# Value means of the first two batches by TensorE products of untransposed values, and 1e-9 added to the early sums on GpSimd

## Chip, cores and metric

The kernel runs on one core of a Trainium2 chip. The metric is the device time of one execution in microseconds, the median of repeated runs. PE is TensorE, DVE is VectorE, ACT is ScalarE, POOL is GpSimd, SP is SyncE, whose queue issues most of the DMAs. An engine carries out its instructions strictly in the order of its queue.

## The reference: what is computed

Four batches, 8 heads, 768 positions, 64 values per head. Attention is a window of 31 positions around each query, joined with 24 summaries of the sequence: of each block of 32 positions the maximum of the keys and the mean of the values. The result goes through an FFN of width 1024: a product with `w_in`, relu, a depthwise convolution of 3 taps, a sigmoid gate, a product with `w_out`.

```python
nb = S // block                                   # 24 blocks of 32
k_sum = k.reshape(B, H, nb, block, D).max(axis=3)
v_sum = v.reshape(B, H, nb, block, D).mean(axis=3)
scores_l_m = np.where(mask_l, scale * q @ k.T, -1e9)
scores_s = scale * np.einsum('bhsd,bhnd->bhsn', q, k_sum) + np.log(block)
scores_all = np.concatenate([scores_l_m, scores_s], axis=-1)
a = np.exp(scores_all - scores_all.max(axis=-1, keepdims=True))
a = a / (np.sum(a, axis=-1, keepdims=True) + 1e-09)
x = np.matmul(a, np.concatenate([v, v_sum], axis=2))
h = np.maximum(x @ w_in, 0.0)
out = (h * sigmoid(conv3(h, conv_w))) @ w_out
```

## The kernel before

The work is cut into 8 chunks: chunk c is one half (384 positions) of batch c // 2. A chunk has 4 head pairs, and two heads of 64 values fill the 128 partitions. `n = 4 * c + p` counts the pairs from 0 to 31. For each pair:

- `prep_pair` (L201): the block maxima of the keys on DVE (`ks`, L209, in the first chunk of a batch), which POOL copies behind the window keys (L216).
- `vmean_pair` (L220), in the first chunk of a batch only: DVE sums the transposed values `vT` over blocks of 32 positions (`vs`, L227, 128 x 768 to 128 x 24), PE transposes the 24 columns into PSUM (`pv`, L233), ACT scales by 1/32 (`vm`, L235). In chunk 0 POOL spreads the means over the six blocks of `va` (L237); later they go there by DMA (L197). Batch 0's `vT` lies in `raw_b`, batches 1 to 3 use a staging tag of two buffers that the loads of `w_out` (L117) use as well.
- `qk` and `softmax` (L247, L270): for each of six blocks of 64 queries and each head one fp32 product of 64 x 120 scores on PE (L259); DVE scales, masks and takes the extreme in one instruction (L277, six per pair); ACT takes the exponential and sums (`sm`, L287, six per pair); ACT adds 1e-9 (L295), DVE takes the reciprocal (L296); the multiply of the weights by it is on DVE for chunk 0 and on POOL afterwards (L299, two per pair).
- `tr` and `av`: six PE transposes of the weights (L307), the copy to `aT` on ACT or DVE (L312, L314), then 12 products with `va` (L328) into `xp`, split into a high part `xh` (ACT) and a rest `xl` (DVE).

The FFN of a chunk has 8 units of 128 columns. `f1` (L403) makes 12 products per unit: four groups of 128 rows times the three combinations of high and low parts of `x` and `w_in`. Relu, taps and gate go to ACT and DVE; the gated result is split into `ghi` (ACT, L454) and `glo` (POOL, L455). `f2` (L471) multiplies by `w_out` the same way. The weights come as 64-bit words and are decoded by ACT and DVE (L96 to L103), split by ACT into the high part (L126) and by POOL into the low part `win_lo` or `wout_lo` (L127).

The attention of chunk c + 1 is woven into the units of chunk c: `slot(j)`, `slot_t(j)` and `slot_av(j)` are called once per unit. The pieces of `f2` are spread over later units by `work`. Around the start PE also runs fillers without use for the result (`warm`, L77, 128 x 512 bf16): 10 first, 5, 12, 3 and 3 behind the scores of chunk 0's pairs, two or three behind its transposes and products and behind chunk 0's units. A scheduler then fixes the order of each engine's queue from estimates of its own, so an edit moves instructions far beyond its own lines. The loads of keys, queries, values and `w_in` are issued on SP in the order of the string `LOADS`; mask and the identity are issued on ACT's queue. Loads for chunk 1 reuse the buffers of chunk 0's pairs and wait for these.

Of the kernel before, what the change touches and what calls it, by code (L numbers as in the profile page):

```python
# [7 lines left out]
F32 = mybir.dt.float32  # L8
F32R = mybir.dt.float32r
U32 = mybir.dt.uint32  # L10
AF = mybir.ActivationFunctionType
ALU = mybir.AluOpType
AX = mybir.AxisListType

B, H, S, D = 4, 8, 768, 64
DM, DF = 512, 1024
P = 128
WIN = 16
BLK = 32
NB = S // BLK  # L20
# [5 lines left out]
NP = H // 2  # L26
CH = S // 2
CB = CH // QB
# [13 lines left out]

OUT_AT = (6, 7, 8, 9, 10, 10, 11, 12)
WARM = {"start": 10, "pq0": 5, "pq1": 12, "pq2": 3, "pq3": 3, "tr": 2, "av": 3, "unit": 3}
EARLY_AT = 3
NGROUP = NCHUNK * NP * 2


@with_exitstack
def attention_ffn(ctx, tc, qT, kT, vT, v4, w_in, cwT, w_out, mask8, ident_in, out):  # L50
    nc = tc.nc
    cp = ctx.enter_context(tc.tile_pool(name="cp", bufs=1))
    sp = ctx.enter_context(tc.tile_pool(name="sp", bufs=2))
# [3 lines left out]
    mask = cp.tile([P, 2, 3, NK], F32, name="mask")  # L57
    ident = cp.tile([P, P], F32, name="ident")
    cw = cp.tile([P, NFC, 3], F32, name="cw")
    win_hi = cp.tile([P, NFC, NCC, P], F32R, name="win_hi")  # L60
    win_lo = cp.tile([P, NFC, NCC, P], F32R, name="win_lo")
    wout_hi = cp.tile([P, NFC, DM], F32R, name="wout_hi")
# [3 lines left out]
    raw_b = cp.tile([P, 6, 1024], U32, name="raw_b", tag="big_b")  # L66
# [7 lines left out]
    def warm(where, after=None):  # L74
        def go():
            for i in range(WARM.get(where, 0)):
                nc.tensor.matmul(pw, idle[:, :P], idle, start=True, stop=True)  # L77
# [55 lines left out]
    state = {}  # L133

    spare = []
    for tag in ("xh", "xl"):
        t = sp.tile([P, 2, KL], F32, tag=tag, name=f"k_{tag}", bufs=2)
# [31 lines left out]
    def load_vt(c, p):  # L169
        b, hf = divmod(c, 2)  # L170
        i = c * NP + p
        if hf:
            return
        if b == 0:
            v = raw_b[:, 2 + p, :S].bitcast(F32)
        else:
            v = sp.tile([P, 1024], F32, tag="stage", name=f"vt{i}", bufs=2)[:, :S]
        nc.sync.dma_start(v, vT[b, p])
        state[(c, p)]["vt"] = v

# [38 lines left out]

    def vmean_pair(c, p):  # L220

        b, hf = divmod(c, 2)
        if hf:
            return
        st = state[(c, p)]
        vs = sp.tile([P, NB], F32, tag="vs", name=f"vs{c}_{p}", bufs=2)
        nc.vector.tensor_reduce(  # L227
            vs, st["vt"].rearrange("p (n t) -> p n t", t=BLK), AX.X, ALU.add
        )
        pv = ps.tile(  # L230
            [P, 512], F32, tag="t" if c else "f1", name=f"pv{c}_{p}", bufs=1 if c else 3
        )
        nc.tensor.transpose(pv[:NB, :P], vs, ident)  # L233
        vm = cp.tile([NB, P], F32, tag=f"vm{p}", name=f"vm{c}_{p}")
        nc.scalar.activation(vm, pv[:NB, :P], AF.Copy, scale=1.0 / BLK)  # L235
        if c == 0:
            nc.gpsimd.tensor_copy(  # L237
                st["va"][WK:NK, :, :], vm.unsqueeze(1).to_broadcast([NB, CB, P])
            )
        state[("vm", b, p)] = vm  # L240
# [6 lines left out]
    def qk(c, p):  # L247


        st = state[(c, p)]  # L250
        n = c * NP + p
        pq = [
            ps.tile([P, 512], F32, tag="s", name=f"pq{n}_{h}", bufs=2) for h in range(2)
        ]
        for blk in range(CB):
            i, half = divmod(blk, 2)
            for h in range(2):
                r = slice(h * QB, (h + 1) * QB)
                last = nc.tensor.matmul(  # L259
                    pq[h][half * QB : (half + 1) * QB, i * NK : (i + 1) * NK],  # L260
                    st["q"][r, blk * QB : (blk + 1) * QB],
                    st["kw"][r, blk, :],
                    start=True,
                    stop=True,
                )
        if c == 0:
            warm(f"pq{p}", ins(last))
        softmax(n, c % 2, pq)

    def softmax(n, hf, pq):  # L270
        nm = sp.tile([P, 2, 3], F32, tag="nm", name=f"nm{n}", bufs=3)
        sm = sp.tile([P, 2, 3], F32, tag="sm", name=f"sm{n}", bufs=3)
        for h in range(2):
            a = sp.tile([P, 3, NK], F32, tag="a", name=f"a{n}_{h}", bufs=DEPTH + 2)
            state[("a", 2 * n + h)] = a
            for i in range(3):
                nc.vector.tensor_tensor_reduce(  # L277
                    a[:, i, :],
                    pq[h][:, i * NK : (i + 1) * NK],
                    mask[:, hf, i, :],  # L280
                    -0.125,
                    3.0e38,
                    ALU.add,
                    ALU.min,
                    nm[:, h, i : i + 1],
                )
                nc.scalar.activation(  # L287
                    a[:, i, :],
                    a[:, i, :],
                    AF.Exp,  # L290
                    bias=nm[:, h, i : i + 1],
                    scale=-1.0,
                    accum_out=sm[:, h, i : i + 1],
                )
        nc.scalar.activation(sm, sm, AF.Copy, bias=1e-9)  # L295
        nc.vector.reciprocal(sm, sm)  # L296
        for h in range(2):
            a = state[("a", 2 * n + h)]
            (nc.gpsimd if n >= NP else nc.vector).tensor_tensor(  # L299
                a, a, sm[:, h, :].unsqueeze(2).to_broadcast([P, 3, NK]), ALU.mult  # L300
            )
# [56 lines left out]
    def slot(j):  # L358

        if j % 2 == 0:  # L360
            n = j // 2 + 2
            if NP <= n < npair:
                load_k(*divmod(n, NP))
                load_vt(*divmod(n, NP))
            if NP <= j // 2 < npair:
                load_vm(*divmod(j // 2, NP))
            if j // 2 < npair:
                qk(*divmod(j // 2, NP))
        else:
            n = (j + 1) // 2  # L370
            if NP <= n + 1 < npair:
                load_q(*divmod(n + 1, NP))
            if n < npair:
                c, p = divmod(n, NP)
                if c:
                    vmean_pair(c, p)
                    load_v(c, p)
                prep_pair(c, p)
# [106 lines left out]
    cw_words = sp.tile([P, 2 * NFC * 3], U32, tag="cww", name="cw_words", bufs=1)  # L485
    nc.scalar.dma_start(mask, mask8)
    nc.scalar.dma_start(ident, ident_in)

    for item in LOADS.split():
        what, n = item[0], int(item[1:] or 0)  # L490
        if what == "k":
            load_k(0, n)
        elif what == "q":
            load_q(0, n)
        elif what == "v":
            load_vt(0, n)
        elif what == "a":
            load_v(0, n)
        elif what == "w":
            raws[n] = load_in(n)  # L500
        else:
            nc.sync.dma_start(cw_words, cwT.bitcast(U32))

    prep_pair(0, 0)
    for j in range(2 * NP):
        slot(j)
        if j % 2 == 0:
            vmean_pair(0, j // 2)
        slot_t(j)
        slot_av(j)  # L510
# [18 lines left out]
    def spread(x, n):  # L529
        return [x[len(x) * i // n : len(x) * (i + 1) // n] for i in range(n)]  # L530

    def work(c):
# [10 lines left out]
        if c == 1:  # L543
            return [[]] * EARLY_AT + spread(parts, NFC - EARLY_AT)
        return spread(parts, NFC)
# [111 lines left out]
```

## Time and profile before

| | |
|---|---|
| median of 3 runs | 415.49 us (414.77 to 416.97) |
| the profiled execution | 414.49 us, its span 412.7 us |
| mean granted clock of TensorE | 0.986 |
| block sums of values (L227) | 16 on DVE: 4 in batch 0 from 8.9 to 24.0 us, 12 from 59.8 to 252.2 us |
| their transposes (L233) | 16 on PE, 0.27 us each as recorded |
| 1e-9 added to the sums (L295) | 32 on ACT, 0.21 us each as recorded |
| fillers (L77) | 85 on PE |

The profile is one execution, recorded on the core. Times are in microseconds from the start of the span unless marked ns. PE is a matmul, PEld its weight load, SPq or ACTq the queue that issues DMAs on that engine. A row of a group reads: line, engine, operation, out<-in, shapes, count | busy time, mean ns of one | idle time of that engine just before them, with what ended it. Matmuls overlap in the pipeline, so the recorded length of one is more than what it adds to a sequence. Rows of the chain have start, duration and what ran; "issue" is time in which nothing shown was waited for.

### The profile page before, as it was taken

The numbers are of one execution on the slowest core, as the hardware profiler recorded it, in microseconds if no ns is written. First come the engines' busy times: TensorE is split into PE (matmuls) and PEld (weight loads), VectorE is DVE, ScalarE is ACT, GpSimd is POOL, SyncE is SP. The second block draws the span as 40 slices with busy tenths as digits, with TensorE's granted clock in tenths as the row PEclk, the third lists the DMA queues.
The fourth block names the chain that finished last, engine by engine and source line by source line (L and its number), as shares of the span: only waits on it lengthen the run. The fifth ranks groups of instructions, "written<-read, shape, count | busy, mean of one in ns | idle before, by whom it ended". The sixth has DMA issues, their size and how long they took to land.

```text
span 412.7 us, 8842 instructions
## 1 busy us (share of the span) xinstructions
PE 395.1 (96%) x3173; PEld 318.4 (77%) x3173; DVE 262.0 (63%) x777; ACT 255.9 (62%) x806; POOL 148.8 (36%) x179
## 2 busy tenths in 40 slices
PE   7989689998999999999999999999999999999996
PEld 3546458775878887888888788887888888888885
DVE  4898989999766756577665454565646655555400
ACT  3664999988695767766556667755666554334211
POOL 2325655565654323332243333333323322212200
PEclk9999999998799999999999999999999999999999
DMA  8999855857976764565332233333111000000011
GB/s 289 331 363 187 241 159 168 241 158 237 218 206 197 231 164 139 151 177 137 84 108 90 78 86 110 111 89 112 54 46 56 27 0 27 25 27 25 28 51 51
DMA packets 60715, 54.47 MB, mean 132 GB/s; under 512 B 24640, under 2 KB 51328, under 8 KB 60672
## 3 DMA queue, kind: packets, MB, share of 16 engines
q1 hardware_dynamic: 56928, 47.19, 40.0%
q10 hardware_dynamic: 3744, 6.73, 4.3%
q8 instruction: 25, 0.41, 0.4%
q14 instruction: 18, 0.15, 0.1%
HBM read 45.55 MB, written 6.29 MB: 126 GB/s over the span
## 4 chain that ended last, share of the span: by engine, by line
PE 74%; ACT 10%; DVE 6%; DMA 3%; POOL 2%; SPq 2%; issue 2%; ACTq 0%; DVEq 0%
PE f L471 30%; PE f L403 28%; PE pq L259 5%; PE xp L328 5%; ACT a L287 4%; PE pt L307 4%; DVE t L433 2%; PE pw L77 2%; DMA va<-v 1%; DMA k_xh<-kT 1%; ACT ob L480 1%; ACT t L424 1%; ACT f L421 1%; ACT aT L314 1%; POOL a L299 1%
## 5 line engine op out<-in xcount | busy, mean ns | idle before, releaser
L455 POOL TENSOR_TENSOR glo<-t,ghi 128x383 fp32r<-128x383 f32 (+1 forms) x64 | 64.9, 1015 | 133.6 <-ACT ghi L454 125.6
L403 PE MATMUL f<-xh,win_hi 128*128 128x384 f32 (+1 forms) x256 | 95.3, 372 | 0.2 <-DVE t L451 0.2
L433 DVE SCALAR_TENSOR_TENSOR t<-f,cw,t 128x382 f32<-128x382 f32 (+3 forms) x128 | 78.7, 615 | 17.1 <-ACT t L424 14.8
L403 PE MATMUL f<-xl,win_hi 128*128 128x384 f32 (+1 forms) x256 | 87.9, 343 | 0.0
L403 PE MATMUL f<-xh,win_lo 128*128 128x384 f32 (+1 forms) x256 | 87.2, 341 | 0.0
L471 PE MATMUL f<-wout_hi,ghi 128*128 128x512 f32 x192 | 79.3, 414 | 1.2 <-ACT ob L480 0.4
L287 ACT ACTIVATE a<-a,nm 128x120 f32<-128x120 f32 x192 | 73.3, 384 | 10.6 <-DVE nm L277 9.9
L471 PE MATMUL f<-wout_lo,ghi 128*128 128x512 f32 x192 | 76.0, 396 | 0.9 <-POOL wout_lo L127 0.8
L471 PE MATMUL f<-wout_hi,glo 128*128 128x512 f32 x192 | 75.3, 392 | 0.0
L450 ACT ACTIVATE t<-t 128x383 f32<-128x383 f32 (+1 forms) x64 | 33.4, 524 | 60.6 <-DVE t L433 60.1
L299 POOL TENSOR_TENSOR a<-a,sm 128x360 f32<-128x360 f32 x56 | 45.9, 840 | 48.3 <-ACT f L421 43.2
L403 PEld LDWEIGHTS f<-xh,win_hi 128*128 128x128 f32 x256 | 48.8, 190 | 7.7 <-issue 3.6
L451 DVE SCALAR_TENSOR_TENSOR t<-t,f 128x383 f32<-128x383 f32 (+1 forms) x64 | 35.4, 553 | 30.2 <-ACT t L450 30.2
L403 PEld LDWEIGHTS f<-xl,win_hi 128*128 128x128 f32 x256 | 49.0, 191 | 1.4
L403 PEld LDWEIGHTS f<-xh,win_lo 128*128 128x128 f32 x256 | 48.7, 190 | 0.4
L471 PEld LDWEIGHTS f<-wout_hi,ghi 128*128 128x128 f32 x192 | 36.1, 188 | 11.6 <-ACT ob L480 3.9
L454 ACT CAST ghi<-t 128x383 fp32r<-128x383 f32 (+1 forms) x64 | 32.8, 512 | 18.5 <-DVE t L451 18.3
L277 DVE CUSTOM_DVE_ANT_0 a<-pq,mask 128x120 f32<-128x120 f32 x192 | 42.4, 276 | 1.5 <-PE pq L259 1.5
L471 PEld LDWEIGHTS f<-wout_hi,glo 128*128 128x128 f32 x192 | 36.2, 188 | 7.8
L471 PEld LDWEIGHTS f<-wout_lo,ghi 128*128 128x128 f32 x192 | 36.2, 189 | 6.9 <-POOL wout_lo L127 1.6
L259 PEld LDWEIGHTS pq<-kw,q 64*64 64x64 f32 x768 | 24.2, 133 | 21.2 <-issue 12.1
L259 PE MATMUL pq<-kw,q 64*64 64x120 f32 x768 | 35.6, 276 | 4.3 <-issue 2.3
(59 smaller groups left out, 508.1 us busy)
## 6 DMA issues: line engine op xcount, KB each, us to landing
va<-v SPq DMA_DIRECT2D x32, 288.0 KB
kw<-kT SPq DMA_DIRECT2D x28, 288.0 KB
q<-qT SPq DMA_DIRECT2D x32, 192.0 KB
out_dram<-ob ACTq DMA_DIRECT2D x24, 256.0 KB
kT<-kT SPq DMA_DIRECT2D x12, 392.0 KB
vt<-vT SPq DMA_DIRECT2D x12, 384.0 KB
wo<-w_out SPq DMA_DIRECT2D x8, 512.0 KB
raw_a<-w_in SPq DMA_DIRECT2D x6, 512.0 KB
```

The source lines that it names most:

```text
L259: last = nc.tensor.matmul(pq[h][half * QB : (half + 1) * QB, i * NK : (i + 1) * NK], st["q"][r, blk * QB : (blk + 1) * QB], st["kw"][r, bl ...
L277: nc.vector.tensor_tensor_reduce(a[:, i, :], pq[h][:, i * NK : (i + 1) * NK], mask[:, hf, i, :], -0.125, 3.0e38, ALU.add, ALU.min, nm[:, h ...
L287: nc.scalar.activation(a[:, i, :], a[:, i, :], AF.Exp, bias=nm[:, h, i : i + 1], scale=-1.0, accum_out=sm[:, h, i : i + 1],)
L299: (nc.gpsimd if n >= NP else nc.vector).tensor_tensor(a, a, sm[:, h, :].unsqueeze(2).to_broadcast([P, 3, NK]), ALU.mult)
L328: last = nc.tensor.matmul(xp[r, blk * QB : (blk + 1) * QB], va[:NK, blk, r], aT[h][:NK, blk * QB : (blk + 1) * QB], start=True, stop=True,)
L403: last = nc.tensor.matmul(ph[:, :n], w[:, fc, cc, :], x[:, cc, :n], start=(cc == 0 and m == 0), stop=(cc == NCC - 1 and m == 2),)
L433: nc.vector.scalar_tensor_tensor(t[:, i0:i1], h[:, hf + k - 1 + i0 : hf + k - 1 + i1], cw[:, fc, k : k + 1], t[:, i0:i1], ALU.mult, ALU.add,)
L450: nc.scalar.activation(t, t, AF.Tanh, scale=0.5)
L451: nc.vector.scalar_tensor_tensor(t, t, 1.0, h[:, hf : hf + ng], ALU.add, ALU.mult)
L454: nc.scalar.copy(hi, t)
L455: nc.gpsimd.tensor_tensor(glo[:, fc, d0 : d0 + ng], t, hi.bitcast(F32), ALU.subtract)
L471: nc.tensor.matmul(po, gx[:, fc, ss], w[:, fc, :], start=(fc == 0 and m == 0), stop=(fc == NFC - 1 and m == 2),)
```

## The change

For batches 0 and 1 (`MEANS_PE = 2`) the values are also loaded untransposed, from `v4`: partition k holds the six consecutive positions 6k to 6k + 5, each with 128 values, which is one run of 3072 bytes per partition. The block sums are then six accumulating fp32 products per pair: for t from 0 to 5 a stationary matrix of 128 x 24 zeros and ones, `ind[:, t, :]`, which says to which block position 6k + t belongs, times the 128 x 128 values. The sums arrive in `pv` where the transpose had put them; the rest of `vmean_pair` is as before. `ind` is a new input of 128 x 144 numbers, loaded by ACT's queue behind mask and identity. Batches 2 and 3 stay as they were.

For the pairs n < 12 (chunks 0, 1 and 2) the 1e-9 is added by a POOL `tensor_scalar` instead of by ACT.

```diff
+MEANS_PE = 2
...
+    ind = cp.tile([P, CB, NB], F32, name="ind")
...
-        if b == 0:
-            v = raw_b[:, 2 + p, :S].bitcast(F32)
-        else:
-            v = sp.tile([P, 1024], F32, tag="stage", name=f"vt{i}", bufs=2)[:, :S]
+        if b < MEANS_PE:
+            if b == 0:
+                v = raw_b[:, 2 + p, :S].bitcast(F32)
+            else:
+                v = sp.tile([P, 1024], F32, tag="stage", name=f"vt{i}", bufs=2)[:, :S]
+            v = v.rearrange("p (t d) -> p t d", d=P)
+            rows = v4[b, p, WIN : WIN + S, :].rearrange("(k t) d -> k t d", t=CB)
+            nc.sync.dma_start(v, rows)
+            state[(c, p)]["vt"] = v
+            return
+        v = sp.tile([P, 1024], F32, tag="stage", name=f"vt{i}", bufs=2)[:, :S]
         nc.sync.dma_start(v, vT[b, p])
...
-        vs = sp.tile([P, NB], F32, tag="vs", name=f"vs{c}_{p}", bufs=2)
-        nc.vector.tensor_reduce(
-            vs, st["vt"].rearrange("p (n t) -> p n t", t=BLK), AX.X, ALU.add
-        )
         pv = ps.tile(
             [P, 512], F32, tag="t" if c else "f1", name=f"pv{c}_{p}", bufs=1 if c else 3
         )
-        nc.tensor.transpose(pv[:NB, :P], vs, ident)
+        if b < MEANS_PE:
+            for t in range(CB):
+                nc.tensor.matmul(
+                    pv[:NB, :P], ind[:, t, :], st["vt"][:, t, :], start=t == 0, stop=t == CB - 1
+                )
+        else:
+            vs = sp.tile([P, NB], F32, tag="vs", name=f"vs{c}_{p}", bufs=2)
+            nc.vector.tensor_reduce(
+                vs, st["vt"].rearrange("p (n t) -> p n t", t=BLK), AX.X, ALU.add
+            )
+            nc.tensor.transpose(pv[:NB, :P], vs, ident)
...
-        nc.scalar.activation(sm, sm, AF.Copy, bias=1e-9)
+        if n < 3 * NP:
+            nc.gpsimd.tensor_scalar(sm, sm, 1e-9, None, ALU.add)
+        else:
+            nc.scalar.activation(sm, sm, AF.Copy, bias=1e-9)
...
     nc.scalar.dma_start(ident, ident_in)
+    nc.scalar.dma_start(ind, ind_in)
...
+    ind = (np.arange(S)[:, None] // BLK == np.arange(NB)).astype(np.float32)
```

The scheduler's order of the queues shifts with it up to chunk 2. Three places follow; in the rows a name's last number is its buffer, and the changed kernel's lines lie further down than those of the kernel before (L276 is L259, L242 is the new product, L313 the new add, L319 is L299, L129 is L127, L226 is L216, L222 is L212, L254 is L237).

The first place is PE's queue behind the five fillers of pair 0's scores, before the change; `pq` are scores, `pw` is the target of the fillers, `pv_0` the means of pair 0.

```order
L77 MATMUL pw<-idle 128x512
L259 MATMUL pq_0_182<-kw_95,q_1_97 64x120 x5
L259 MATMUL pq_1_183<-kw_95,q_1_97 64x120 x5
L259 MATMUL pq_0_182<-kw_95,q_1_97 64x120
L259 MATMUL pq_1_183<-kw_95,q_1_97 64x120
L77 LDWEIGHTS idle
L77 MATMUL pw<-idle 128x512
L233 MATMUL pv_0_173<-ident,vs_0_171 24x128
```

The transposed sums come last here. The same place after the change:

```order
L79 LDWEIGHTS idle
L79 MATMUL pw<-idle 128x512
L242 MATMUL pv_0_173<-raw_b,ind 24x128 x6
L276 MATMUL pq_0_187<-kw_97,q_1_99 64x120
L276 MATMUL pq_1_188<-kw_97,q_1_99 64x120
```

The means of pair 0 were one transpose behind the scores of pair 1 and a filler; they are six products ahead of all scores of pair 1.

The second place is POOL's queue at the start, before the change; `kw` are keys, `va` values with means, `sm` the sums of the softmax; a row that says only ISA is the compiler's own, ahead of POOL's first arithmetic.

```order
L237 COPY va_104<-vm_0_175 24x768
L212 COPY kw_107<-k_xl 128x6x96
L237 COPY va_111<-vm_1_232 24x768
L216 COPY kw_107<-ks_331 128x6x24
L237 COPY va_116<-vm_2_298 24x768
L237 COPY va_120<-vm_3_386 24x768
L127 ISA
L127 TENSOR_TENSOR win_lo<-wu_i_485,win_hi 128x512
```

The ISA row stands ahead of the first `win_lo`, behind the copies for all four pairs. After the change:

```order
L313 ISA
L313 TENSOR_SCALAR sm_154<-sm_154 128x6
L254 COPY va_106<-vm_0_180 24x768
L313 TENSOR_SCALAR sm_214<-sm_214 128x6
L254 COPY va_113<-vm_1_240 24x768
L222 COPY kw_109<-k_xl 128x6x96
L226 COPY kw_109<-ks_342 128x6x24
L313 TENSOR_SCALAR sm_283<-sm_283 128x6
L254 COPY va_118<-vm_2_309 24x768
L129 TENSOR_TENSOR win_lo<-wu_i_499,win_hi 128x512
L313 TENSOR_SCALAR sm_374<-sm_374 128x6
```

The four early adds stand among the copies, the ISA row has moved to the first of them, and the first `win_lo` is ahead of the add of pair 3 (`sm_374`).

The third place is POOL's queue around the first multiplies of chunk 1 (`a_0`, `a_1` are the weights of a pair's heads), before the change:

```order
L127 TENSOR_TENSOR win_lo<-wu_i_627,win_hi 128x512
L299 TENSOR_TENSOR a_0_540<-a_0_540,sm_539 128x360
L299 TENSOR_TENSOR a_1_547<-a_1_547,sm_539 128x360
L127 TENSOR_TENSOR win_lo<-wu_i_635,win_hi 128x512
L299 TENSOR_TENSOR a_0_582<-a_0_582,sm_581 128x360
L299 TENSOR_TENSOR a_1_589<-a_1_589,sm_581 128x360
L127 TENSOR_TENSOR win_lo<-wu_i_701,win_hi 128x512
```

Multiplies and low parts of weights alternate. After the change:

```order
L129 TENSOR_TENSOR win_lo<-wu_i_628,win_hi 128x512
L129 TENSOR_TENSOR win_lo<-wu_i_641,win_hi 128x512
L129 TENSOR_TENSOR win_lo<-wu_i_649,win_hi 128x512
L226 COPY kw_577<-ks_342 128x6x24
L129 TENSOR_TENSOR win_lo<-wu_i_715,win_hi 128x512
L313 TENSOR_SCALAR sm_553<-sm_553 128x6
L319 TENSOR_TENSOR a_0_554<-a_0_554,sm_553 128x360
L319 TENSOR_TENSOR a_1_561<-a_1_561,sm_553 128x360
L313 TENSOR_SCALAR sm_595<-sm_595 128x6
L319 TENSOR_TENSOR a_0_596<-a_0_596,sm_595 128x360
L319 TENSOR_TENSOR a_1_603<-a_1_603,sm_595 128x360
```

Of the eight `win_lo`, one used to stand behind the multiplies of each of the pairs 4, 5 and 6; now seven are ahead of the first multiply, and each pair's multiplies follow its add.

More of the change, by code (lines that the diff above doesn't have):

```diff
@@ L49, in attention_ffn @@
 @with_exitstack
-def attention_ffn(ctx, tc, qT, kT, vT, v4, w_in, cwT, w_out, mask8, ident_in, out):
+def attention_ffn(ctx, tc, qT, kT, vT, v4, w_in, cwT, w_out, mask8, ident_in, ind_in, out):
     nc = tc.nc
@@ L645 @@
         "ident": np.eye(P, dtype=np.float32),
+        "ind": ind.reshape(P, CB, NB),
     }
```

## The prediction

> **What bounds the kernel now.** I read the page first: its totals, its clock row, and the chain of work that ended last, by engine.
>
> ```profile
> span 412.7 us, 8842 instructions
> PE 395.1 (96%) x3173; PEld 318.4 (77%) x3173; DVE 262.0 (63%) x777; ACT 255.9 (62%) x806; POOL 148.8 (36%) x179
> PEclk9999999998799999999999999999999999999999
> PE 74%; ACT 10%; DVE 6%; DMA 3%; POOL 2%; SPq 2%; issue 2%; ACTq 0%; DVEq 0%
> ```
>
> Over the whole span PE is the bound, and a change that gives PE more work to spare DVE and ACT should cost time. But that is an average over stages. The windows by stage (columns: length, then busy time of PE, PEld, DVE, ACT and POOL, the granted clock, the DMA share, GB/s) say where it doesn't hold.
>
> ```profile
> 0.00:31.00 31.00, 26.81 (x246) 14.03 (x246) 23.61 (x84) 17.03 (x68) 8.65 (x17) 0.97 1.00 327
> 31.00:58.00 27.00, 20.92 (x231) 14.63 (x229) 24.30 (x75) 20.30 (x67) 16.69 (x17) 0.97 0.90 223
> 58.00:83.00 25.00, 25.00 (x247) 19.45 (x244) 23.70 (x68) 22.92 (x76) 14.31 (x19) 1.00 0.57 175
> 83.00:103.00 20.00, 17.91 (x152) 13.68 (x150) 19.38 (x51) 17.63 (x54) 11.67 (x13) 0.94 0.64 196
> 103.00:131.00 28.00, 27.47 (x188) 23.11 (x187) 20.02 (x56) 20.49 (x61) 15.72 (x17) 0.92 0.79 202
> 131.00:163.00 32.00, 31.68 (x278) 26.14 (x277) 19.83 (x64) 22.41 (x74) 11.55 (x15) 1.00 0.61 184
> 163.00:385.00 222.00, 221.31 (x1746) 188.00 (x1746) 128.74 (x381) 130.50 (x401) 68.20 (x83) 1.00 0.26 77
> ```
>
> From 163 us on PE is busy throughout and DVE and ACT have four tenths to spare: nothing can be won there, and the work of that part is not changed. Up to 103 us DVE is the fullest engine or next to it: 24.30 of 27 us, 23.70 of 25, 19.38 of 20. The eight reductions that go, the twelve small ACT steps and the added matmuls nearly all lie in this part, so the forecast is a sum over 0 to 131 us. The chain in order of time (start, duration, what) shows how the opening runs.
>
> ```profile
> 8.63 1.33 PE pq L259 x22
> ...
> 10.39 2.38 PE pw L77 x11
> ...
> 15.45 0.56 DVE aT L312
> 16.01 0.99 DVE a L299 x2
> 16.99 0.19 DVE a L277
> ...
> 17.23 2.38 ACT a L287 x12
> ...
> 19.97 0.12 ACT sm L295
> ...
> 23.11 2.38 ACT a L287 x12
> ...
> 25.84 0.11 ACT sm L295
> ```
>
> Until 15.4 us it runs through PE, with its fillers; then through the softmax of pairs 2 and 3, where each exponential batch of 2.38 us is followed by the sum step, the reciprocal and the multiply.
>
> **The change, part by part.** The rows of the groups by shape (duration in ns after the comma) price what goes and what comes.
>
> ```profile
> L259 PE MATMUL pq<-kw,q 64*64 64x120 f32 x768 | 35.6, 276 | 4.3 <-issue 2.3 <-DVE nm L277 1.1 <-POOL kw L216 0.9
> L216 POOL COPY kw<-ks 128x144 f32<-128x144 f32 x32 | 11.6, 363 | 31.0 <-PE pq L259 22.9 <-DVE ks L209 7.7 <-POOL glo L455 0.3
> L227 DVE TENSOR_REDUCE vs<-vt 128x24 f32<-128x768 f32 x12 | 11.4, 948 | 0.8 <-PE pv L233 0.7
> L295 ACT ACTIVATE sm<-sm 128x6 f32<-128x6 f32 x32 | 6.6, 206 | 0.0
> L233 PE MATMUL pv<-ident,vs 128*24 128x128 f32 x16 | 4.4, 274 | 0.0
> L227 DVE TENSOR_REDUCE vs<-raw_b 128x24 f32<-128x768 f32 x4 | 3.8, 944 | 0.0
> ```
>
> *Reductions.* All four from raw_b (batch 0) and four of the twelve from vt (batch 1) go: 8 x 0.95 = 7.6 us of DVE, 3.8 in each half of the opening.
>
> *Added matmuls.* One pair's means were one transpose and become six plain fp32 products of 128 columns. A plain fp32 product leaves two records (384 score products stand as 768 in the row), a transpose one (16 of 16). What a record costs in sequence is read from the chain, not from the 274 ns, which overlaps its neighbours:
>
> ```profile
> 63.73 0.33 PE pt L307 x3
> 69.13 0.85 PE xp L328 x24
> 174.32 1.06 PE f L403 x6
> ```
>
> A record of 128 columns takes 0.33 / 3 = 0.11 us, so a pair's means cost 12 x 0.11 = 1.3 us in place of 0.11: +1.2 us per pair. Bounds: 12 x 0.035 = 0.4 us by the 64-column xp record, 12 x 0.177 = 2.1 us by the 384-column f record. I take 1.2, by the row of the same width. Eight pairs give +9.6 us of PE, half in the opening, half between 58 and 103 us.
>
> *Where they stand at the start.* The order puts the six products of pair 0 ahead of pair 1's scores and those of pair 1 ahead of pair 2's, in front of the first transposes of weights. PE was on the chain there, so +2.4 us until aT at 15.45. Some is given back: the multiply of pair 1 (0.99) and pair 2's first score step (0.19) now stand ahead of that aT copy on DVE, so 1.2 us no longer follow it. Term 1: +1.2 us. Bounds: -0.2, if the products are pulled into gaps; +4.0, if pair 0's products hold PE's queue until their untransposed values and the 0/1 matrix (a DMA new on ACT's queue, behind mask and ident) have landed.
>
> *Reductions that had cover.* The third and fourth of batch 0 lay at
>
> ```profile
> 18.13 0.94 DVE L227 TENSOR_REDUCE vs<-raw_b 128x24 f32<-128x768 f32 x1
> 24.00 0.94 DVE L227 TENSOR_REDUCE vs<-raw_b 128x24 f32<-128x768 f32 x1
> ```
>
> inside the two ACT batches of 17.23 to 19.61 and 23.11 to 25.49. On the softmax chain they were free; what they held up is the decode of w_in, which the new order draws into those slots.
>
> *31 to 58 us.* Here DVE is 90% busy with that decode and chunk 1's scores, and the chain pays for late decode twice over:
>
> ```profile
> 48.28 0.11 ACT sm L295
> 48.39 0.52 ACT win_hi L126
> 48.90 0.07 issue
> 48.97 1.53 POOL win_lo L127
> ```
>
> These 2.2 us lie between two multiplies of pairs 4 and 5. In the new order of POOL seven of the eight win_lo stand ahead of the first of these multiplies. Term 2: -3.8 us, the DVE time of batch 0's reductions. Bounds: 0, if the DMA (share 1.00 and 0.90 in the first two windows) sets when this stage can start; -6.0 with the 2.2 us.
>
> *The sums' 1e-9 on POOL.* ACT loses 12 steps of 0.11 to 0.12 us net. POOL gains 12 operations on 128x6 and the chain one more handover (0.07 by the row at 48.90). No row shows POOL on so little: the 144-column copy of 0.36 us is the upper bound, nothing the lower; I take 0.3. On the chain: 0.3 + 0.07 - 0.12 = +0.25 us for each of the two batches at 19.97 and 25.84. The reciprocal on DVE now waits for POOL, and behind it in DVE's queue stand the multiplies of batch 0, xl and the gate's steps; ahead of some adds stands a glo or a win_lo in POOL's queue. Term 3: +0.5 us; bounds 0 and +2.0 (one win_lo of 1.53 ahead of one add that is waited for).
>
> The first add matters also for a load of code: the order shows a library row of POOL ahead of its first arithmetic, which was the first win_lo and is now the first add.
>
> ```profile
> 30.18 1.74 POOL L127 TENSOR_TENSOR win_lo<-wu_i,win_hi 128x512 fp32r<-128x512 f32 x1 [3.11 <-ACT win_hi L126]
> ```
>
> There POOL had been idle for 3.11 us, ended by ACT, so a load of up to that length would have been hidden. I take nothing for it. The Trainium skill (GPSIMD Engine Reference, 2.1 Instruction dispatch) says that the first call of a freshly loaded kernel pays about 6 us with no instruction in the profile; the sum by that page would be 6 us worse, and this trace shows no such gap.
>
> *58 to 103 us.* DVE gives back 3.8 us, ACT 8 x 0.11 = 0.9 us, PE takes 4 x 1.2 = 4.8 us. In 58 to 83 us all three are over nine tenths busy, so there the gain and the price of three pairs (2.8 against 3.6) nearly cancel. The loads of w_out wait for the reductions to give their staging buffer back,
>
> ```profile
> SPq L117 <- DVE vs L227: 10.1, 3, 4.6
> ```
>
> 10.1 us in three waits; they will wait for PE's products instead, which stand in PE's order after the value products of the pair before, so I expect no earlier load. In 83 to 103 us PE waits while DVE decodes w_out between scores, and the clock falls afterwards:
>
> ```profile
> 88.37 1.06 DVE wl_o L99
> ...
> 103.32 4.16 PE f L403 x12
> ```
>
> Twelve f records took 4.16 us in place of 2 x 1.06. An earlier decode shortens both. Term 4: -1.6 us (+0.8 in the first of the two stages; in the second -0.9 for the fourth reduction and -1.5 of the 2.0 us of slow clock). Bounds: -5.9 (3.8 of DVE and the 2.0 of the slow clock), +2.7 (PE's 4.8 less the 2.1 it has free in 83 to 103).
>
> *103 to 131 us.* Four adds of chunk 2 stand behind glo in POOL's queue. Term 5: +0.3; bounds 0 and +1.0.
>
> Loads keep their sizes, since a partition reads 3072 bytes in either layout; the matrix adds 72 KB, 0.2 us at 327 GB/s. From unit 3 of chunk 2 on the orders agree again, which costs nothing.
>
> **The sum.** +1.2 - 3.8 + 0.5 - 1.6 + 0.3 = -3.4 us. The profiled execution took 414.49 us, 1.79 around its span, so it would take 411.1. It was 1.0 us under the median of the three runs, 415.49; for a median I say 412.1 us.
>
> **The rivals.** *PE is the bound already (0.22).* Nothing is given back at aT (+2.4), chunk 1 starts no earlier because its value loads wait for chunk 0's products (term 2 at 0), and in 58 to 103 us the products outweigh their free time (4.8 - 2.1 = +2.7). With terms 3 and 5: +5.9, 421.4 us. For it: PE on the chain until 15.4 and 25.00 of 25 in the third window. Against it: fillers are part of that, and DVE is as full. It decides where a pair's products pass about 1.5 us.
>
> *Nothing to measure (0.26).* The start is set by DMA (share 1.00 and 0.90), so terms 1 to 3 come to nothing, and the gain of 58 to 103 is paid back: 415.5 us within 2. For it: the bandwidth of 327 GB/s. Against it: DVE's 24.30 of 27 us with the share already down.
>
> *Code loading (0.06).* As forecast, but the load at the first add is exposed by the 3.11 us that had hidden it: 415.2 us. That page's rule, in full, would give 418.1.
>
> The change does what it says: the order shows it, and I give no chance to the opposite.
>
> **How the numbers follow.** The forecast has 0.46. About 0.5%, 2.1 us, can be told from no change here: faster is below 413.4, slower above 417.6. The forecast's own range, 406.5 to 414.5, gives 0.40 faster and 0.06 same; nothing-to-measure 0.04, 0.18 and 0.04; code loading 0.04 same and 0.02 slower; PE-bound 0.03 same and 0.19 slower. Together 0.44, 0.31, 0.25. The range that leaves out one in ten on each side is 406.5 to 419.5.
>
> **What would show it.** Right: first transposes of weights near 15.5 us but the first continuous f records before 57; win_lo done ahead of the first multiply on POOL; DVE's busy time under 21 us in 58 to 83. Wrong: a means group of over 1.5 us on PE, POOL's add over 0.5 us or with an idle stretch of microseconds ahead of the first, or the stretch from 163 us to the end longer than before.

## The result, and the profile after

The changed kernel takes 420.61 us (median of 4 runs, 419.61 to 422.26) where the kernel before took 415.69 us beside it: a ratio of 1.0111 with a 95% interval of 1.0076 to 1.0146. It is slower, by 4.6 us by that ratio (the two medians lie 4.9 us apart); 3.4 us less had been forecast. Executions over 1.5% above the fastest of their kernel are left out of the ratios here. The changed kernel's totals, clock row and chain by engine, in the form shown before:

```profile
span 418.7 us, 9008 instructions
PE 397.3 (95%) x3251; PEld 322.2 (77%) x3261; DVE 254.8 (61%) x769; ACT 256.2 (61%) x794; POOL 152.4 (36%) x191
PEclk9989999999999999999999999999999999999999
PE 66%; ACT 11%; DVE 11%; DMA 7%; POOL 2%; issue 2%; ACTq 0%; DVEq 0%
```

DVE lost 7.2 us of work, as it should, and the clock no longer dips near 105 us (a smaller dip lies between 21 and 31 us now). Yet the span is 6.0 us longer. The windows by stage, in the same cuts as before:

```profile
0.00:31.00 31.00, 22.56 (x208) 12.59 (x212) 16.02 (x61) 12.94 (x48) 8.57 (x19) 0.94 1.00 302
31.00:58.00 27.00, 22.93 (x230) 15.91 (x232) 24.70 (x81) 18.18 (x60) 16.46 (x18) 1.00 0.74 190
58.00:83.00 25.00, 24.53 (x251) 19.15 (x254) 17.61 (x53) 22.39 (x71) 13.58 (x21) 1.00 0.70 178
83.00:103.00 20.00, 19.69 (x197) 16.52 (x196) 17.36 (x53) 18.13 (x55) 12.45 (x16) 1.00 0.81 237
103.00:131.00 28.00, 24.82 (x202) 19.14 (x202) 25.39 (x72) 22.24 (x67) 15.96 (x16) 1.00 0.74 210
163.00:385.00 222.00, 221.14 (x1765) 187.50 (x1766) 129.31 (x392) 133.36 (x417) 70.18 (x86) 1.00 0.27 80
```

In the first window PE, DVE and ACT all did less than before (DVE 16.02 us where it had been 23.61, more than the 3.8 us removed): work was pushed back. In 58 to 83 us DVE now has seven tenths to do and PE is nearly as full as it was (24.53 us of 25): the relief arrived there, and the table of marks below shows no unit that starts earlier for it. The chain of the changed kernel, with a row of PE's timeline for the wait that it shows:

```profile
10.67 10.21 DMA raw_b<-v
20.88 0.04 issue
20.92 0.59 PE pv L242 x2
21.51 0.83 PE pt L327 x3
...
67.38 1.42 PE pv L242 x12
...
391.01 23.93 PE f L491 x105
```

```profile
20.92 0.59 PE L242 MATMUL pv<-raw_b,ind 128*24 128x128 f32 x2 [4.92 <-DMA raw_b<-v]
```

PE stood still for 4.92 us ahead of the products of pair 2, whose values were issued at 10.67 and landed at 20.88; the first transposes of weights, which stand behind the first of those products in PE's queue, came at 21.4 us instead of 13.04. The last 105 products of f2 start at 391.01 us, against 385.08 before, 5.9 us late, and they last 23.93 us in both; the row of before:

```profile
385.08 23.93 PE f L471 x105
```

Where the 5.9 us arose is seen by following one mark through the two timelines of PE, the first f1 product of a unit (chunk.unit, in us; worked out by counting the f1 records, 12 to a unit):

```
unit      0.0    0.1    0.2    0.5    1.0    1.4    2.0    3.0    7.0
before   33.5   37.6   45.5   65.8   78.3  103.3  128.6  174.1  353.0
after    36.0   46.1   55.9   72.8   88.1  108.4  134.5  180.1  359.0
late by   2.5    8.5   10.4    7.0    9.8    5.2    5.9    6.0    5.9
```

From chunk 2 on the distance is fixed. Everything happens before 130 us: an opening that runs up to 10 us behind, of which a part is regained later. The drop from 9.8 to 5.2 us goes with a new order of f2's products: of these PE ran 13 records between 82 and 104 us before and none after, and at unit 2.0 both kernels have done 48 (counted in the two timelines). That timeline alone suggests that the blocked queue of the opening is the cause. The experiments say otherwise.

### The profile page after: what moved, and what is told of

Its sections match the earlier page's. It is cut to its first block, busy times and chain, and to the rows that moved or that the text cites. A ratio compares the mean times of both kernels' runs of the same rounds, so it can differ in the third digit from the quotient of the medians.

```text
span 418.7 us, 9008 instructions
## 1 busy us (share of the span) xinstructions
PE 397.3 (95%) x3251; PEld 322.2 (77%) x3261; DVE 254.8 (61%) x769; ACT 256.2 (61%) x794; POOL 152.4 (36%) x191
## 4 chain that ended last, share of the span: by engine, by line
PE 66%; ACT 11%; DVE 11%; DMA 7%; POOL 2%; issue 2%; ACTq 0%; DVEq 0%
PE f L491 29%; PE f L423 24%; ACT a L304 5%; PE xp L348 5%; PE pt L327 4%; PE pq L276 3%; DMA raw_b<-v 2%; DVE t L453 2%; DMA kT<-kT 2%; DMA k_xl<-kT 1%; ACT ob L500 1%; ACT f L441 1%; DVE wu_o L105 1%; DMA vt<-vT 1%; DMA mask<-mask 1%
## 5 line engine op out<-in xcount | busy, mean ns | idle before, releaser
L423 PE MATMUL f<-xl,win_hi 128*128 128x384 f32 (+1 forms) x256 | 86.9, 340 | 0.0
L319 POOL TENSOR_TENSOR a<-a,sm 128x360 f32<-128x360 f32 x56 | 45.1, 826 | 43.0 <-ACT f L441 41.6
L446 DVE TENSOR_SCALAR t<-f,cw 128x385 f32<-128x385 f32 (+1 forms) x32 | 19.8, 620 | 26.7 <-ACT f L441 26.5
L304 ACT ACTIVATION_READ_ACCUMULATOR a<-a,nm 128x1 f32 x192 | 35.9, 187 | 0.0
```

The lines of the kernel that those rows point to most:

```text
L304: nc.scalar.activation(a[:, i, :], a[:, i, :], AF.Exp, bias=nm[:, h, i : i + 1], scale=-1.0, accum_out=sm[:, h, i : i + 1],)
L319: (nc.gpsimd if n >= NP else nc.vector).tensor_tensor(a, a, sm[:, h, :].unsqueeze(2).to_broadcast([P, 3, NK]), ALU.mult)
L423: last = nc.tensor.matmul(ph[:, :n], w[:, fc, cc, :], x[:, cc, :n], start=(cc == 0 and m == 0), stop=(cc == NCC - 1 and m == 2),)
L446: nc.vector.tensor_scalar(t, h[:, hf : hf + ng], cw[:, fc, 1:2], 1.0, ALU.mult, ALU.mult)
```

## The experiments

Ratios are to the kernel before, run beside it on the same chip, with 95% intervals.

```
what was changed                                              ratio
the change                                                    1.0111 (1.0076 to 1.0146)
products of batches 0 and 1, no adds on POOL                  1.0132 (1.0055 to 1.0208)
adds on POOL only                                             1.0061 (1.0029 to 1.0093)
the change, batch 0's products read the identity              1.0135 (1.0097 to 1.0173)
the change, batch 0's products tied behind transposes         1.0258 (1.0198 to 1.0318)
before, with the load of the matrix                           1.0007 (0.9980 to 1.0034)
the change, matrix and identity in one load                   1.0154 (1.0095 to 1.0213)
the same, no adds on POOL                                     1.0107 (1.0048 to 1.0165)
products of batch 1 only (one load, no adds)                  1.0093 (1.0056 to 1.0130)
products of batch 1, each twice                               1.0204 (1.0163 to 1.0244)
batch 1 without reductions and without products               1.0022 (0.9990 to 1.0053)
products of batch 0 only (one load, no adds)                  1.0025 (0.9993 to 1.0058)
adds on POOL for chunks 1 and 2 only                          1.0002 (0.9977 to 1.0028)
adds on POOL for chunk 0 only                                 1.0072 (1.0042 to 1.0102)
the change without the adds of chunk 0                        1.0115 (1.0065 to 1.0164)
before, without the fillers behind units                      0.9913 (0.9878 to 0.9949)
the change, without the fillers behind units                  1.0317 (1.0271 to 1.0364)
```

### The blocked queue, the added work, or the adds

The first theory was the one that the chain suggests, that the wait for pair 2's values in PE's queue is the loss; the rivals were PE's added work and the handover to POOL. First the products without the adds.

```diff
-        if n < 3 * NP:
+        if n < 0:
             nc.gpsimd.tensor_scalar(sm, sm, 1e-9, None, ALU.add)
```

> The 1e-9 stays on ACT for all pairs; the means of batches 0 and 1 are products as in the change. In the order of PE's queue the first transposes of weights then stand ahead of the products of pair 2. Three theories. Queue theory (the changed kernel loses its time because the products of pair 2, which wait 4.9 us for their values, stand ahead of pair 0's transposes in PE's queue): the first transposes come at 14 to 16 us instead of 21.4, and the time is 413 to 416 us. Work theory (the 9.6 us of added products are the loss): 420 us as in the change. Hand-over theory (the add on POOL is the loss, by its own time and its handover): 413 to 416 us too, so this run parts only the work theory from the others.

The first transposes came at 16.4 us and PE's wait for the values shrank to 0.6 us, as the queue theory wanted, and the time stayed: 1.0132. The wait can't be the whole loss. The opening was late all the same, though: unit 0.2 started at 51.9 us, against 45.5 before and 55.9 in the change. The granted clock is a rival that these runs leave open: in the mean of the executions it was 0.992 in the change and 0.984 here, so a part of what the wait gave back may have gone to a lower clock.

Then the adds without the products:

```diff
-MEANS_PE = 2
+MEANS_PE = 0
```

(with batch 0's transposed values in `raw_b` as before).

> All means by reductions on DVE as before; only the twelve adds are on POOL. In the order of DVE's queue the reduction of pair 2, which needs the same late values, now stands ahead of pair 0's multiplies. Queue theory: DVE waits there for pair 2's values until 18 to 21 us, the first transposes come after 19 us in place of 13.0, and the time is 417 to 421 us although nothing was added to PE. Work theory: 415.5 us, as before. Hand-over theory: 418 to 421 us, with waits of the reciprocal on POOL's adds of several us in all and no long wait on the DMA.

1.0061 of 415.5 us is 418.0, inside the queue theory's range, and its mark is there: the first transposes came at 22.1 us, and the waits of DVE and PE on this kernel name the late values. Columns are us in total, times, longest.

```profile
PE pv L248 <- DVE vs L245: 6.2, 2, 6.0
DVE vs L245 <- DMA raw_b<-vT: 5.4, 2, 4.5
```

With the add on POOL the scheduler placed pair 2's reduction ahead of pair 0's multiplies, and DVE waited there for the DMA; the multiplies began at 21.47 us instead of 11.90. So the adds have a price, and it needs no product.

The change with its wait taken away by other data:

```diff
-                    pv[:NB, :P], ind[:, t, :], st["vt"][:, t, :], start=t == 0, stop=t == CB - 1
+                    pv[:NB, :P], ind[:, t, :], st["vt"][:, t, :] if c else ident, start=t == 0, stop=t == CB - 1
```

> As the change, adds on POOL too, but the six products of each pair of chunk 0 read the identity in place of the values, so batch 0's block means are left out and PE never waits for its values; the loads are still made. Queue theory: the wait of 4.9 us goes, first transposes at 15 to 17 us, 413 to 416.5 us. Work theory: the products are all there, 420 us. Hand-over theory: the adds are all there, 420 us.

1.0135. PE waited 2.7 us once, for the matrix, and never for values; nothing was won. But the first transposes still came at 20.5 us, not at 15 to 17: with the data at hand, the new order put still more products ahead of them. So this run speaks against the wait itself as the loss, and says nothing of an opening that isn't late.

The change with batch 0's products put later by hand, tied behind the transposes of the same pair:

```diff
         slot(j)
-        if j % 2 == 0:
-            vmean_pair(0, j // 2)
         slot_t(j)
+        if j % 2 == 0 and j >= 2:
+            vmean_pair(0, j // 2 - 1)
         slot_av(j)
...
+        if j == 2 * NP:
+            vmean_pair(0, NP - 1)
```

(the tie itself is not shown).

> As the change, all products and adds kept, but in chunk 0 the products of a pair are written behind the transposes of that pair's first head and tied behind them in PE's queue. Queue theory: 411 to 416 us, first transposes by 14.5 us. Work theory and hand-over theory: 419 to 421 us.

1.0258, worse than every theory. The first transposes came at 16.9 us, but the means are now late for the pair's own product with `va`, and the loads of chunk 1's values wait for that product (SP's wait, columns as above).

```profile
SPq L203 <- PE xp L351: 7.6, 1, 7.6
```

Since it brought a delay of its own, this run decides between no two theories; it shows that this remedy isn't one.

### One more load

Reading the loads' issue times gave another theory. In the changed kernel SP issued the third pair's keys 2 us later, and waited for the mask with it (SP's timeline before, the same after, and the wait after: us in total, times, longest):

```profile
3.10 0.46 SPq L163 DMA_DIRECT2D k_xl<-kT  x1
```

```profile
5.16 0.33 SPq L165 DMA_DIRECT2D k_xl<-kT  x1
```

```profile
SPq L165 <- DMA mask<-mask: 2.0, 1, 2.0
```

Before, it was the load after it that waited for the mask. In both kernels eight loads had been issued by then, six on SP and two on ACT before, five and three after, and the ninth waited. The test adds nothing but that load to the kernel before:

```diff
     nc.scalar.dma_start(ident, ident_in)
+    nc.scalar.dma_start(ind, ind_in)
```

> The kernel before with one thing added: the load of the 128 x 144 matrix on ACT's queue behind the identity; nothing reads it, and the order of the engines' queues is that of the kernel before. Slot theory (loads wait for the eighth load before them to land, so one more load at the head makes each load of the opening wait for a later one): the third pair's keys are issued at 5.0 us instead of 3.10 and wait for the mask, the first load of chunk 1 at about 25 us instead of 23.3, and the time is 2 to 4 us over the kernel before. Work theory and queue theory: 72 KB more, 0.2 us, no change that can be told.

The keys moved to 5.00 us as foreseen, and the time did not move: 1.0007. The delay is real and hidden. The reverse, the change with the matrix and the identity as one input:

```diff
-    nc.scalar.dma_start(ident, ident_in)
-    nc.scalar.dma_start(ind, ind_in)
+    nc.scalar.dma_start(both, both_in)
```

> The whole change, but the matrix and the identity come as one input in one load, so the number of loads is that of the kernel before. Slot theory: the third pair's keys are issued by 3.5 us again, and the time is 2 to 4 us under the change, 416 to 418.5 us. Work theory: 420 us. Queue theory: 418 to 420 us, since the products of pair 2 still stand ahead of the first transposes, only with an earlier landing.

The keys were back at 3.15 us and the time was 1.0154, no better. This theory is out. The next run takes the adds away as well.

> As the run before with the 1e-9 back on ACT, so all products of batches 0 and 1, no added load, no add on POOL. Slot theory: 3 to 5 us under the same kernel with its own load of the matrix (1.0132 of the kernel before there), so 0.998 to 1.005 of it here. Work theory: 1.010 to 1.014.

That one, with one load for both inputs and the 1e-9 on ACT, gave 1.0107: neither the added load nor the adds, and the loss is still there. What is left in it is the products and the order that comes with them.

### The dose

Batch 1 alone leaves the opening as it was:

```diff
-        if b < MEANS_PE:
+        if b == 1:
```

(in both places, with the one load and the 1e-9 on ACT; for batch 0 the values come transposed as before).

> Products for batch 1 alone, batch 0 on DVE as before, 1e-9 on ACT, matrix and identity in one load: the opening is that of the kernel before. Slot theory: 0.99 to 1.00 of the kernel before, with the w_out stretch of 88 to 103 us shortened as in the change. Work theory (4.8 us of products on PE): 1.005 to 1.012.

1.0093: nearly the whole loss, in a kernel whose first transposes come at 13.5 us and whose unit 0.2 starts at 45.4 us, as before. Two more doses, at the same place:

```diff
-            for t in range(CB):
+            for t in range(2 * CB):
                 nc.tensor.matmul(
-                    pv[:NB, :P], ind[:, t, :], st["vt"][:, t, :], start=t == 0, stop=t == CB - 1
+                    pv[:NB, :P], ind[:, t % CB, :], st["vt"][:, t % CB, :], start=t == 0, stop=t == 2 * CB - 1
                 )
```

> Products for batch 1 alone as in the run with batch 1 alone (1.0093 of the kernel before), but twelve for a pair instead of six, each value counted twice and the scale halved: 4.8 us more of PE and nothing else. Work theory (PE is the bound between 60 and 130 us, its added time counts there nearly one for one): 1.017 to 1.024. Order theory (it is the reshuffled queues that cost, not PE's time): 1.006 to 1.012.

and none at all, with the reductions gone too:

```diff
-            vs = sp.tile([P, NB], F32, tag="vs", name=f"vs{c}_{p}", bufs=2)
-            nc.vector.tensor_reduce(
-                vs, st["vt"].rearrange("p (n t) -> p n t", t=BLK), AX.X, ALU.add
-            )
+            vs = st["vt"][:, :NB]
```

(for batch 1).

> Batch 1's four reductions are left out and no products put in their place: the transpose reads 24 columns of the values, so batch 1's block means are left out. DVE is relieved as in the change, PE does what it did before. This is the gain side alone. Forecast as on record (DVE's time counts between 58 and 103 us): 0.992 to 0.997. Work theory: DVE is not the bound, so 0.997 to 1.003. Order theory: 1.004 to 1.010.

The ratios are 1.0022, 1.0093 and 1.0204 for 0, 6 and 12 products a pair. At 417 us the first six cost 3.0 us and the next six 4.6 us, for 5.2 and 5.7 us of PE (48 records more at 1.42 / 12 = 0.118 us, by the chain above, are 5.7; the first step also saves four transposes of 0.11). By the intervals each of the two costs is known to about 2 us. The windows of the three kernels over 58 to 131 us, in that order and with the columns of before:

```profile
58.00:131.00 73.00, 69.97 (x580) 55.81 (x578) 59.60 (x169) 61.12 (x190) 41.57 (x47) 0.98 0.67 192
```

```profile
58.00:131.00 73.00, 67.91 (x582) 54.75 (x584) 53.92 (x160) 56.78 (x179) 39.92 (x44) 0.94 0.61 176
```

```profile
58.00:131.00 73.00, 67.54 (x595) 55.82 (x598) 54.21 (x151) 55.18 (x169) 38.79 (x44) 0.93 0.59 173
```

These need care. The time grows from the first to the last, yet PE, the engine that was given more to do, is less busy: a window of fixed time holds less of the work the later a kernel runs. Cut at the same work instead, from the start of unit 0.2 to that of unit 2.0, each of the three timelines holds the same 672 PE records, with 44 more for six products (48, less the four transposes) and 92 more for twelve (in us; worked out from the timelines):

```
products per pair      0      6     12
from 0.2 to 2.0     83.0   89.1   93.9
PE busy in it       76.1   80.8   86.4
PE idle in it        6.9    8.3    7.6
granted clock       0.98   0.93   0.93
```

The step from six to twelve is at an equal clock: 48 records more make PE 5.6 us busier and the stretch 4.8 us longer. The step from none to six isn't, so its 6.1 us are in part the clock of that one execution. Over all executions the clock doesn't explain the ratios: its mean was 0.987, 0.987 and 0.984 for the three kernels. Executions with the same mean clock of 0.984 took 418.4 and 419.1 us without products, 420.4 to 422.2 with six and 425.0, twice, with twelve. DVE's busy time in the stretch is 69.8, 67.0 and 69.0 us, so DVE has room in all three.

And the first of the runs is the gain side by itself: four reductions out of DVE, PE unburdened, and 1.0022 with an interval from 0.9990. Of 3.8 us of DVE at most 0.4 us came back, in the order that the scheduler then made of it.

Batch 0 alone:

> Products for batch 0 alone, 1e-9 on ACT, identity and matrix in one load. Work theory: the products of batch 0 run where PE has fillers and waits, so 1.000 to 1.004. Queue theory (products that wait for late values hold PE's queue in the opening): 1.006 to 1.012.

1.0025, no difference that can be told, although PE waited 1.8 us for values and unit 0.2 started at 51.3 us instead of 45.5. Unit 2.0 started at 130.0 us, 1.4 late: most of the delay was made up by then. An opening that is late by 6 us need not cost.

### Whose adds

```diff
-        if n < 3 * NP:
+        if NP <= n < 3 * NP:
```

> No products, reductions as before; the adds on POOL for chunks 1 and 2 only, ACT keeps those of chunk 0; identity and matrix in one load. The opening's order is that of the kernel before. If the cost of the adds alone (1.0061) came from the opening's order, where the scheduler drew pair 2's reduction ahead of pair 0's multiplies: 0.997 to 1.002. If it came from the handover and from POOL's queue: 1.004 to 1.008.

1.0002, with an interval that allows 1 us either way: the eight adds of chunks 1 and 2 cost nothing that can be told, queue and handover included. The other four:

```diff
-        if n < 3 * NP:
+        if n < NP:
```

> No products; the adds on POOL for chunk 0's four pairs only; identity and matrix in one load. If the adds cost through the opening's order (pair 2's reduction, which waits for its values, ahead of pair 0's multiplies on DVE): 1.003 to 1.009 as with all twelve. If not: 0.998 to 1.002.

1.0072, with the same waits as in the run with all twelve:

```profile
PE pv L249 <- DVE vs L246: 6.1, 2, 5.7
DVE vs L246 <- DMA raw_b<-vT: 4.9, 2, 4.2
```

So the price of the adds is that of chunk 0's. That it comes by the order that they bring about is read from these waits; no run has the four adds without the new order. In the change itself there is no reduction left to wait there; this is the change without chunk 0's adds:

> The change with the adds of chunk 0 back on ACT, so that the first transposes stand ahead of pair 2's products. If the prices add up (products of batch 1 0.9%, of batch 0 0.2%, chunk 0's adds 0.6%): 1.005 to 1.010. If the products make the opening's order no matter: 1.010 to 1.014.

It took 1.0115, with its first transposes at 15.2 us and unit 0.2 at 49.1 instead of 55.9. So a much earlier opening won nothing that can be told, which is the clearest evidence against the queue theory, and the price of chunk 0's adds is not one that the change pays on top. The parts, 0.9%, 0.2% and 0.7%, add up to more than the whole of 1.1% (the intervals are 0.3 to 0.4 wide on each side); whether the opening's share vanishes in the whole, and why, wasn't settled.

### Taking PE work out

```diff
-WARM = {"start": 10, "pq0": 5, "pq1": 12, "pq2": 3, "pq3": 3, "tr": 2, "av": 3, "unit": 3}
+WARM = {"start": 10, "pq0": 5, "pq1": 12, "pq2": 3, "pq3": 3, "tr": 2, "av": 3, "unit": 0}
```

> The kernel before without the 24 fillers behind the units of chunk 0 (24 x 0.22 = 5.3 us of PE, 15 of them in 58 to 83 us). Work theory (PE is the bound there whatever it does): 3 to 5 us less, 0.987 to 0.995, unless the granted clock falls in that stretch. If PE only looks full because fillers pad its waits: 0.998 to 1.003.

0.9913: 3.6 us won from 5.3 us of fillers, by an edit that takes work from PE alone. But the orders of all engines changed with it, and the clock did too: its mean over the executions was 0.990, against 0.983 of the kernel before beside it, so a part of the 3.6 us may be clock. The gain fits a PE that is the bound there by its work, fillers included, and it doesn't prove it. The windows of this kernel:

```profile
58.00:83.00 25.00, 23.52 (x219) 19.72 (x219) 21.66 (x71) 21.52 (x71) 13.16 (x18) 0.96 0.52 157
83.00:103.00 20.00, 16.70 (x159) 13.12 (x158) 18.63 (x48) 17.68 (x57) 12.17 (x14) 1.00 0.95 226
```

This is a version faster than both kernels. The same edit on the changed kernel should then have given its loss back:

> The changed kernel without the same 24 fillers. Work theory: the products of batch 1 take the fillers' place, 0.998 to 1.004 of the kernel before instead of 1.0111. If fillers are padding: 1.008 to 1.014.

It gave 1.0317, a miss for both theories: the work theory's own test failed here. The chain of that run shows another order with another stall, POOL's queue this time:

```profile
106.42 0.98 POOL sm L313
...
107.48 1.01 POOL glo L475
108.49 2.39 POOL a L319 x2
110.88 1.25 POOL wout_lo L129
112.17 1.22 PE f L491 x2
```

```profile
L491 PE MATMUL f<-wout_lo,ghi 128*128 128x512 f32 x5 | 3.0, 596 | 4.2 <-POOL wout_lo L129 4.2
```

The low part of a w_out block stood behind an add, a glo and two multiplies on POOL; f2's products waited 4.2 us for it on PE (their group between 105 and 128 us), and the window of 113 to 118 us had a granted clock of 0.50. Here the add is in the queue that hurts, but whether the add or the new order did it wasn't tried. Nor is the stall the whole loss: the execution in which it was profiled took 424.18 us, the shortest of five, and the others took up to 432.50 us at granted clocks down to 0.964.

## Why the prediction was wrong

The step that failed is term 4. The prediction put DVE's time of batch 1 on the path between 58 and 103 us at its full value and let it nearly cancel PE's products in the first of the two stages, where PE stood at 25.00 of 25 us; in the second it charged PE's fourth pair nothing. The runs show one side only: DVE's relief there is worth nothing that can be told (1.0022), and PE's added time counts by six to eight tenths (3.0 us of 5.2, 4.6 of 5.7). Term 2 failed too, by less. Set against the parts that were timed alone, at 417 us:

```
                                  forecast   measured (95% interval)
terms 1 and 2, batch 0              -2.6      +1.0 (-0.3 to +2.4)
terms 3 and 5, the adds             +0.8      +2.5 (+1.2 to +3.9)
term 4, batch 1                     -1.6      +3.9 (+2.3 to +5.4)
the whole                           -3.4      +4.6 (+3.2 to +6.1)
```

The rival "PE is the bound already", given 0.22, had that mechanism and 421.4 us, against 420.61. It had the right reason in its last part (+2.7 us, where the runs show 3.9) and too much in the first (+2.4 for batch 0, where they show 1.0), so that its total came out this close is partly luck.

Point by point:

- *Price of a product.* Estimated 1.3 us a pair, measured 1.42 in the chain (row at 67.38): right, and the bound of 2.1 us was not needed.
- *Term 1, +1.2 us with an upper bound of 4.0.* The first transposes came 8.4 us late. The bound had the wait on values in it, but for pair 0; it was pair 2's values that landed late, and the order of PE's queue, with one of pair 2's products ahead of the first transposes and one between them, had said which. On the total this counted for little: batch 0's products alone cost 1.0025.
- *Term 2, -3.8 us.* Not there. With batch 0's reductions gone (and its products on PE) unit 0.2 started at 51.3 us instead of 45.5 and the time was 1.0025; the forecast took a DVE that is 90% busy for a DVE that sets the end. No run takes these four reductions away without putting products in their place, so why term 2 came to nothing is less sure than term 4.
- *Terms 3 and 5, the add on POOL.* The group of the adds and the first of them in POOL's timeline:

```profile
L313 POOL TENSOR_SCALAR sm<-sm 128x6 f32<-128x6 f32 x12 | 2.9, 246 | 24.7 <-ACT a L304 24.6
```

```profile
11.31 0.69 POOL L226 COPY kw<-ks 128x144 f32<-128x144 f32 x2
12.09 0.24 POOL L313 TENSOR_SCALAR sm<-sm 128x6 f32<-128x6 f32 x1
```

  One takes 0.24 us, where 0.3 was taken, and no code load is seen: the first add begins 0.1 us behind the copies ahead of it. The 6 us of the Trainium skill (GPSIMD Engine Reference, 2.1 Instruction dispatch) are not in this trace, nor the 3.1 us of the rival. What the term missed is that the add on POOL for chunk 0's pairs makes the scheduler put other work first; alone that costs 0.7%.
- *Loads.* That the loads of w_out would wait for PE's products instead of the reductions, and no less long, was right (10.1 us in three waits before):

```profile
SPq L119 <- PE pv L242: 9.5, 2, 7.2
```

- *Clock.* The dip from 103 us went, as term 4 had hoped (0.92 became 1.00 in 103 to 131 us), without gain in the whole. The first products of f2, which had stood among the waits from 82 us on, start at 104.0 us now, and PE has to do them later. That a wait for DVE's decode is one that PE could afford is the reading that fits; no run tried it alone.
- *What would show it.* The prediction's mark for right, DVE under 21 us in 58 to 83, was met (17.61) by a slower kernel. It was a mark of the edit, not of the gain. None of the three marks for wrong came: a means group took 1.42 us, an add 0.24 us, and from unit 3.0 to the end both profiles take 238.6 us. The list had no mark for a PE that is the bound between 58 and 103 us.
- *A sum.* The lower bound of term 4, -5.9, is -5.8 by its two figures; nothing hangs on it.

## What to carry to other kernels

Where three engines are over nine tenths busy in a stage, busy time doesn't say which of them counts. Take work out of each in turn and time it: here a version without batch 1's reductions (DVE) would have shown, before a matrix product was written, that there was nothing to win, and one without the fillers (PE) would have pointed at PE. Compare profiles between the same marks of the work, not between the same times. And where a scheduler orders the queues, price an edit with the order that it causes: four adds of 0.24 us cost 3 us where the new order had a reduction that waits for a DMA ahead of work that was ready.

## What was not expected of the hardware

One profiled execution can be off by most of what is looked for. The kernel before with the extra load has the same order of PE, DVE, POOL and SP and a ratio of 1.0007, yet its profiled span was 415.9 us against 412.7; unit 0.5 started 3.9 us later in it. Of the 6.0 us between the two profiles of before and after, 4.6 are found by timing.

SP's issue of a load waited for an earlier one to land, the mask at about 5 us, once eight loads were out; with one more load on ACT's queue the wait came one load earlier on SP. It moved the keys of the third pair by 1.9 us and the total by nothing.
